# First batch of a fused attention and feed-forward kernel: k and v loaded as two blocks

## The chip, the cores and the metric

One core of a Trainium2 chip runs the whole program. The metric is device time in microseconds (us), a median of several executions. The engines run side by side and wait for each other by semaphores: TensorE (PE in the profile, its weight loads PEld), VectorE (DVE), ScalarE (ACT), GpSimd (POOL) and SyncE (SP). Loads are started by instructions in the queues of SP and ACT and are carried out by 16 DMA engines.

## The reference

For each of 8 batches and 8 heads (576 positions, head size 64, 32 memory slots):

```python
a = exp(phi - max(phi, axis=2));  a = a / (sum(a, axis=2) + 1e-9)
k_m = einsum('bhsm,bhsd->bhmd', a, k)          # 32 x 64 per head
v_m = einsum('bhsm,bhsd->bhmd', a, v)
attn = softmax(q @ k_m.T / sqrt(64))            # 576 x 32 per head
x = (attn @ v_m)  -> rows of 8 * 64 = 512       # 4608 x 512
h = x @ w_in;  g = h * sigmoid(h)               # 4608 x 2048
out = g @ w_out                                 # 4608 x 512
```

## The kernel before, in words

The batches are worked one after the other. For each, the softmax weights of phi are exponentials `e`; matmuls with `e` as weights sum k, v and a column of ones into 32 rows per head (`e_mm`), so that the ones give the sum to divide by. The scores come from q and k's sums, and are turned, exponentiated and normed. v's sums are not multiplied with the scores but with w_in (`p_mm`), and the result is the weight of the first matrix multiplication of the feed-forward part (`ffn1`, line 637). `silu` and `ffn2` (line 676) follow, 16 steps of 128 columns of h for a batch. In steady state TensorE does 12 matmuls of `ffn1` and 12 of `ffn2` for each step, and all that prepares the next batch lies beside them.

The start is written out by hand, from line 768 on, and the change is there. The order of the instructions of TensorE, VectorE, ScalarE and SP is fixed as written (`in_order`). Nothing of the feed-forward part can run before batch 0 has gone through the attention, and the loop for batch 0 also loads and converts the rest of the weights. The weights come as 64-bit words; `w_conv` makes float32 of them in steps that are single letters: "p" and "c" on ScalarE, "s" and "a" on VectorE, for w_out also "h" and "l". `keep_warm` issues matmuls whose result nobody reads.

The steps that the prediction names, in the order of the code:

- `load_phi`, `load_kv`: phi in three pieces; k, v and ones of batch 0 interleaved in one array, 129 columns for each head and position, four loads of 516 KB (128 positions each) and one of 258 KB (the last 64 positions, `kr`), all on ACT's queue.
- `LOADS` (line 43): the loads after these, on SP's queue: i0 and i1 are the first two 128-column blocks of w_in (512 KB each), Q0 and Q1 the halves of q (576 KB each), o0 and o1 blocks of w_out (512 KB each), L the next weights in a list. Each of them waits until the load five places before it has landed (`DEEP`).
- `phi_max` to `phi_exp`: the exponentials of the two head groups p = 0 and p = 1, in this order.
- `e_mm(0)`: for p = 0, then p = 1, 16 matmuls of 129 columns (lines 318 to 323), and 16 for the last 64 positions (line 330); then the sums of the ones, their reciprocals (`rs`), and the scaled k and v (`kvn`).
- `f_tr`, `f_vt`: transposes of k's and v's part of `kvn`, copied by VectorE and ScalarE into `kvT`.
- `f_scores(u)`, `f_copy(u)`, `f_turn(u)` for the two halves u of q: scores (line 480), copies to SBUF (`sT`, `sleft`), transposes back (`firstu`).
- `f_max`, `f_sub`, `f_exp`, `f_sum`, `f_norm`, `f_back`, `f_high`, `f_low`: the softmax and its split into two parts, `aparts`. `f_high(1)` is the last that the first matmuls of `ffn1` wait for.
- `p_mm(0, 0)` needs v's part of `kvT` and the converted i0 and i1.

The lines that set the order around the change:

```python
LOADS = "i0 Q0 Q1 i1 o0 o1 L L L"
...
        e_mm(0)
        w_conv(I0, 0, "pc")
        keep_warm(idle, 3)
        f_tr()
        f_vt()
...
        f_scores(1)
        f_max(0)
        f_copy(1)
        f_sub(0)
        keep_warm(spare, 3)
        f_turn(1)
```

Of the kernel before, what the change touches and what calls it, by code (L numbers as in the profile page):

```python
# [10 lines left out]
F32 = mybir.dt.float32  # L11
# [4 lines left out]
AF = mybir.ActivationFunctionType  # L16
ALU = mybir.AluOpType
AX = mybir.AxisListType

P = 128  # L20
B, S, H, M, D = 8, 576, 8, 32, 64
# [17 lines left out]

PHW = FULLC * HM + P  # L40
KVC = 2 * NR * KVW
RAWB = 3
LOADS = "i0 Q0 Q1 i1 o0 o1 L L L"
HOMES = {("o", 1): 8, ("i", 2): 12}
DEEP = 5

# [2 lines left out]
def attn_ffn_kernel(  # L49
    ctx: ExitStack,  # L50
    tc: tile.TileContext,
    phi: bass.AP,
    kv: bass.AP,
    qT: bass.AP,
    w_in: bass.AP,
# [126 lines left out]
    def load_next(few=False):  # L182
        w = next(to_load, None)
        if w is not None:
            w_load(w, None, few)
# [35 lines left out]
    def load_kv(b):  # L221
        queue = nc.scalar if b == 0 else None
        ts = []
        for c in range(FULLC):
            t = sb.tile([P, 2, NR, KVW], F32, tag="kv", name=f"kv{b}_{c}", bufs=FULLC)
            load(t.rearrange("p g r f -> p (g r f)"), kv[b, :, c * KVC : (c + 1) * KVC], queue=queue)
            ts.append(t)
        t = sb.tile([P, NR, KVW], F32, tag="kr", name=f"kr{b}", bufs=1)
        load(t.rearrange("p r f -> p (r f)"), kv[b, :, FULLC * KVC :], queue=queue)
        at[b]["kv"], at[b]["kr"] = ts, t  # L230

    def load_q(b, hf, few=False):
        t = sb.tile([P, NR, HALF], F32, tag="q", name=f"q{b}_{hf}", bufs=2)
        at[b]["q", hf] = t
        load(t.rearrange("p r s -> p (r s)"), qT[b, hf], few)
# [78 lines left out]
    def e_mm(b):  # L314
# [26 lines left out]
        for p in range(2):  # L341
# [3 lines left out]
            else:  # L345
                nc.vector.tensor_scalar(kvn[:, :, p], src, rs[p], None, op0=ALU.mult)

    def e_tr(b):
        pt = beside_h(P)
        t = sb.tile([P, 2, NR, M], F32, tag="kvT", name=f"kvT{b}", bufs=2)  # L350
        for kind in range(2):
            nc.tensor.transpose(pt[kind], kvn[:, kind].rearrange("p g d -> p (g d)"), ident)  # L352
        nc.vector.tensor_copy(t[:, 0].rearrange("p r m -> p (r m)"), pt[0])
        nc.scalar.copy(t[:, 1].rearrange("p r m -> p (r m)"), pt[1])
        at[b]["kvT"] = t
# [100 lines left out]
    def f_tr():  # L456
        pt = ps.tile([P, 512], F32, tag="acc", name="firstt", bufs=NI)
        t = sb.tile([P, 2, NR, M], F32, tag="kvT", name="kvT0", bufs=2)
        at[0]["kvT"] = t
        for kind in range(2):  # L460
            nc.tensor.transpose(
                pt[:, P * kind : P * (kind + 1)], kvn[:, kind].rearrange("p g d -> p (g d)"), ident
            )
        nc.vector.tensor_copy(t[:, 0].rearrange("p r m -> p (r m)"), pt[:, :P])
        first["vt"] = t, pt

    def f_vt():
        t, pt = first["vt"]
        nc.scalar.copy(t[:, 1].rearrange("p r m -> p (r m)"), pt[:, P : 2 * P])

    def f_scores(u):
        if u == 0:
# [15 lines left out]
    def f_copy(u):  # L488
        if u == 0:
            first["left"] = sb.tile([P, P], F32, tag="mx", name="sleft", bufs=1)  # L490
        t = first["main", u] = sb.tile([P, 2, 2 * P], F32, tag="kv", name=f"sT{u}", bufs=FULLC)
        left = first["left"].rearrange("p (g h f) -> p g h f", g=2, h=2)[:, :, u]
        st = first["st", u]
        if u:
            nc.scalar.copy(t, st[:, :, : 2 * P])
            nc.scalar.copy(left, st[:, :, 2 * P : HALF])
            return
        nc.scalar.copy(t[:, 0], st[0][:, : 2 * P])
        nc.vector.tensor_copy(t[:, 1], st[1][:, : 2 * P])
        for p in range(2):  # L500
            nc.scalar.copy(left[:, p], st[p][:, 2 * P : HALF])
# [43 lines left out]
    def f_exp(u):  # L545
        nc.scalar.activation(f_sc(u), f_sc(u), AF.Exp, scale=SCALE)
# [221 lines left out]
    with in_order(DVE, ACT) as last:  # L768
        load_phi(0)
        nc.scalar.activation(tiny[:, :1], ident[:, :1], AF.Exp)  # L770
        load_kv(0)
        for c in LOADS.split():
            if c[0] == "Q":
                load_q(0, int(c[1]), True)
            elif c[0] == "L":
                load_next(True)
            else:
                w_load((c[0], 0), int(c[1]), True)
        keep_warm(idle, 10)
# [7 lines left out]
        for p in range(2):  # L787
            phi_exp(0, (p,))
        keep_warm(idle, 2)
        e_mm(0)  # L790
        w_conv(I0, 0, "pc")
        keep_warm(idle, 3)
        f_tr()
        f_vt()
        w_conv(I0, 0, "s")
        keep_warm(idle, 2)
        f_scores(0)
# [6 lines left out]
        f_max(0)  # L804
        f_copy(1)
        f_sub(0)
        keep_warm(spare, 3)
        f_turn(1)
        f_exp(0)
        w_conv(I0, 1, "pc")  # L810
        f_max(1)
        f_sub(1)
        f_exp(1)
        nc.scalar.activation(tiny[:, :1], ident[:, :1], AF.Silu)
        keep_warm(spare, 13)
        f_sum(0)
        f_norm(0)
        w_conv(I0, 1, "sa")
# [110 lines left out]
def layout(q, k, v, phi, moe_w_in, moe_w_out):  # L929
# [7 lines left out]
        ],  # L937
        axis=2,
    )
    ph = phi.reshape(B, NR, 2, S, M).transpose(0, 3, 2, 1, 4).reshape(B, S, 2, P)  # L940
    ph = np.concatenate(
        [
# [10 lines left out]
    qT = q[:, :, cols].reshape(B, NR, 2, 2, HALF, D).transpose(0, 3, 2, 5, 1, 4).reshape(B, 2, P, NR * HALF)  # L953
    return {
        "in_phi": np.ascontiguousarray(ph),
        "in_kv": np.ascontiguousarray(kv),
        "in_q": np.ascontiguousarray(qT),
        "in_w_in": np.ascontiguousarray(moe_w_in).view(np.int64),
# [12 lines left out]
```

## Time and profile before

| | us |
|---|---|
| median of 3 runs | 701.22 (701.16 to 701.29) |
| the profiled execution | 702.12 |
| its span, first to last instruction | 700.3 |
| TensorE busy in it | 689.4 |
| VectorE busy | 365.4 |
| ScalarE busy | 259.0 |

Times in the rows below are microseconds from the span's start, unless ns stands beside them. The profiled execution is 0.90 us longer than the median of the runs.

### The profile page before, as it was taken

Reading aid. Unit: us, or ns where it says so; the run is one execution under the profiler, and the core shown is the slowest. Engines: PE = TensorE matmul, PEld = TensorE weight load, DVE = VectorE, ACT = ScalarE, POOL = GpSimd, SP = SyncE. Lnnn points to the kernel's source line nnn. Section 1 sums busy time; section 2 is a strip of 40 time slices with the busy share of each in tenths; the row PEclk is TensorE's granted clock in tenths of the full one; section 3 lists DMA queues with packets and bytes.
Section 4 is the critical chain, followed back from the end, with each engine's and each line's share of the span. In section 5 each row is a group of like instructions: output and inputs, shape, how many; then the busy total and the mean of one; then the engine's idle time right before and its main releaser. Section 6 shows DMA issues by size and latency. Waiting matters only on the chain.

```text
span 700.3 us, 11773 instructions
## 1 busy us (share of the span) xinstructions
PE 689.4 (98%) x4924; PEld 562.4 (80%) x4924; DVE 365.4 (52%) x665; ACT 259.0 (37%) x456; POOL 0.7 (0%) x6
## 2 busy tenths in 40 slices
PE   7999999999999999999999999999999999999997
PEld 3578777888888888888888888888888888888886
DVE  4898797435654256534636346542564525623322
ACT  3879584422424224421423314342241413431211
POOL 0000000000000000000000000000000000000000
PEclk9999999999999999999999999999999999999999
DMA  9995752212201221132110311112121000010002
GB/s 334 317 338 187 254 212 95 78 61 68 92 19 46 92 68 44 52 137 69 35 61 16 137 56 47 61 54 83 68 80 31 1 1 1 1 61 1 1 0 76
DMA packets 25445, 60.15 MB, mean 86 GB/s; under 512 B 2096, under 2 KB 10416, under 8 KB 25392
## 3 DMA queue, kind: packets, MB, share of 16 engines
q1 hardware_dynamic: 24448, 56.63, 22.8%
q10 hardware_dynamic: 944, 2.77, 1.1%
q8 instruction: 39, 0.64, 0.4%
q14 instruction: 14, 0.11, 0.1%
HBM read 49.95 MB, written 9.44 MB: 85 GB/s over the span
## 4 chain that ended last, share of the span: by engine, by line
PE 84%; DVE 2%; issue 0%; ACT 0%; ACTq 0%
PE acc L676 45%; PE h L637 25%; PE accleft L676 6%; PE bg L602 4%; PE h L322 2%; PE bg L367 1%; DVE wo_lo L176 0%; DVE raw L172 0%; PE h L330 0%; PE h L352 0%; DVE aparts L448 0%; DVE aT L442 0%; DVE gparts L654 0%; DVE sc L415 0%; DVE smx L411 0%
## 5 line engine op out<-in xcount | busy, mean ns | idle before, releaser
L676 PE MATMUL acc<-wo_hi,gparts 128*128 128x512 f32 x1024 | 341.8, 395 | 0.1
L676 PEld LDWEIGHTS acc<-wo_hi,gparts 128*128 128x128 f32 x1024 | 192.0, 188 | 52.7 <-issue 6.6
L637 PEld LDWEIGHTS h<-aparts,pparts 128*128 128x128 f32 x1524 | 214.0, 188 | 14.4 <-issue 2.1
L637 PE MATMUL h<-aparts,pparts 128*128 128x288 f32 x1524 | 223.3, 295 | 0.7 <-ACT aparts L581 0.4
L660 ACT ACTIVATE g<-h 128x512 f32<-128x512 f32 x127 | 76.0, 599 | 345.9 <-PE h L637 180.3
L676 PE MATMUL acc<-wo_lo,gparts 128*128 128x512 f32 x512 | 200.8, 392 | 0.7 <-DVE wo_lo L176 0.6
L652 DVE CAST gparts<-g 128x512 fp32r<-128x512 f32 x128 | 54.4, 425 | 260.0 <-ACT g L660 260.0
L676 PEld LDWEIGHTS acc<-wo_lo,gparts 128*128 128x128 f32 x512 | 96.1, 188 | 18.4 <-DVE wo_lo L176 1.9
L654 DVE TENSOR_TENSOR gparts<-g,gparts 128x512 fp32r<-128x512 f32 x128 | 88.2, 689 | 10.3
L618 DVE TENSOR_TENSOR pparts<-bg,pparts 128x1024 fp32r<-128x1024 f32 (+1 forms) x36 | 39.7, 1102 | 5.4 <-ACT pparts L616 5.0
L676 PE MATMUL accleft<-wo_hi,gparts 128*128 128x512 f32 x128 | 40.6, 389 | 0.0
L616 ACT ACTIVATE pparts<-bg 128x1024 fp32r<-128x1024 f32 (+1 forms) x36 | 33.6, 932 | 14.8 <-PE bg L602 14.8
L602 PE MATMUL bg<-win,kvT 64*32 64x512 f32 (+1 forms) x576 | 35.8, 554 | 0.0
L676 PEld LDWEIGHTS accleft<-wo_hi,gparts 128*128 128x128 f32 x128 | 24.0, 188 | 4.9
L662 ACT ACTIVATE gleft<-h 128x64 f32<-128x64 f32 x127 | 27.8, 219 | 0.0
L683 ACT ACTIVATE o<-acc 128x512 f32<-128x512 f32 x32 | 19.2, 600 | 21.8 <-PE acc L676 10.6
L676 PE MATMUL accleft<-wo_lo,gparts 128*128 128x512 f32 x64 | 24.9, 389 | 0.0
L660 ACT ACT_TABLE_LOAD x14 | 18.0, 1283 | 14.2 <-issue 13.6
L652 DVE CAST gparts<-gleft 128x512 fp32r<-128x512 f32 x16 | 6.8, 427 | 20.7 <-PE accleft L676 12.2
L168 ACT ACTIVATE raw<-raw 128x1024 int32<-128x1024 uint32 (+1 forms) x16 | 16.8, 1048 | 0.0
L322 PEld LDWEIGHTS h<-kv,phi 128*32 128x32 f32 x384 | 10.2, 110 | 5.0 <-ACT gleft L662 5.0
L676 PEld LDWEIGHTS accleft<-wo_lo,gparts 128*128 128x128 f32 x64 | 12.0, 188 | 2.4
(139 smaller groups left out, 365.0 us busy)
## 6 DMA issues: line engine op xcount, KB each, us to landing
kv<-in_kv SPq DMA_DIRECT2D x28, 516.0 KB, 5.9
q<-in_q SPq DMA_DIRECT2D x16, 576.0 KB, 5.7
out<-o SPq DMA_DIRECT2D x32, 256.0 KB, 2.1
raw<-in_w_in SPq DMA_DIRECT2D x14, 512.0 KB, 6.6
raw<-in_w_out SPq DMA_DIRECT2D x6, 1024.0 KB, 5.5
phi<-in_phi SPq DMA_DIRECT2D x7, 576.0 KB, 3.8
kv<-in_kv ACTq DMA_DIRECT2D x4, 516.0 KB, 6.8
kr<-in_kv SPq DMA_DIRECT2D x7, 258.0 KB, 6.4
```

What stands on the lines that cost most here:

```text
L168: nc.scalar.activation(r, low, AF.Copy, scale=2.0**-29)
L322: nc.tensor.matmul(pt[p][M * r : M * (r + 1), :KVW], e[:, p, c, M * r : M * (r + 1)], kvt[c][:, p, r], start=c == 0, stop=False, skip_grou ...
L602: nc.tensor.matmul(bg[M * r : M * (r + 1), p, :w].rearrange("p (k f) -> p k f", f=P), kvT[D * p : D * (p + 1), 1, r], win[D * p : D * (p + ...
L616: nc.scalar.activation(hi[:, :, c], bg[:, :, :w], AF.Copy)
L618: nc.vector.tensor_tensor(lo[:, :, c], bg[:, :, :w], hi[:, :, c], op=ALU.subtract)
L637: nc.tensor.matmul(h[:, hf, :HALF], wt[:, p, fs], a[:, p, hf * HALF : (hf + 1) * HALF], start=n[hf] == 0, stop=n[hf] == 5, skip_group_chec ...
L652: nc.vector.tensor_copy(ghi, g32)
L654: last_split.append(nc.vector.tensor_tensor(glo, g32, ghi, op=ALU.subtract))
L660: nc.scalar.activation(g32.rearrange("p (h f) -> p h f", h=2), h[:, :, :w], AF.Silu)
L662: i = nc.scalar.activation(gleft[:, fc, o : o + LEFT].rearrange("p (h f) -> p h f", h=2), h[:, :, w:HALF], AF.Silu)
L676: nc.tensor.matmul(acc[key], gt[:, cs], wt[:, fc], start=fc == 0 and n == 0, stop=fc == NFC - 1 and n == 2)
L683: nc.scalar.activation(o, a, AF.Copy)
```

## The change

For batch 0 alone, the host lays out a second array of k and v, `kv0`: all of k with its column of ones first (four blocks of 128 positions, then the last 64), then all of v. The loads write into the same tiles as before, k's part ahead of v's part in each. k's five loads (four of 260 KB, one of 130 KB) take the place of the five on ACT's queue. v's five (four of 256 KB, one of 128 KB) go on SP's queue at the place V of `LOADS`, and wait like the others there for the load five places before. The order on SP becomes Q0, i0, Q1, v, i1 and on.

`e_mm(0)` becomes `e_first(0)`, which sums k and the ones (65 columns), and two calls of `e_first(1)`, which sum v (64 columns): p = 0 between `f_scores(1)` and `f_turn(1)` where three `keep_warm` matmuls were, p = 1 behind `f_turn(1)`. Each is 16 matmuls and 4 for the last positions. `k_first` makes `rs` and k's `kvn`, for p = 0 on VectorE and for p = 1 on ScalarE; `v_first` scales v on ScalarE for both p, behind `w_conv(I0, 1, "pc")`. `f_tr` has one transpose. `f_vt` has v's, on TensorE behind three `keep_warm` matmuls after `f_exp(1)`, and its copy on ScalarE ahead of the tiny Silu activation. The 13 `keep_warm` matmuls there become 6. The copies `sT` get other buffers, those that the conversion of w_out uses later.

```diff
--- before.py
+++ after.py
@@ -39,8 +39,11 @@
 
 PHW = FULLC * HM + P
 KVC = 2 * NR * KVW
+KW = D + 1
+KC = 2 * NR * KW
+K0 = FULLC * KC + NR * KW
 RAWB = 3
-LOADS = "i0 Q0 Q1 i1 o0 o1 L L L"
+LOADS = "Q0 i0 Q1 V i1 o0 o1 L L L"
 HOMES = {("o", 1): 8, ("i", 2): 12}
 DEEP = 5
 
...
@@ -228,6 +232,24 @@
         t = sb.tile([P, NR, KVW], F32, tag="kr", name=f"kr{b}", bufs=1)
         load(t.rearrange("p r f -> p (r f)"), kv[b, :, FULLC * KVC :], queue=queue)
         at[b]["kv"], at[b]["kr"] = ts, t
+
+    def kv0_parts(t, n):
+
+        f = t.rearrange("p g r f -> p (g r f)") if n == 2 * NR else t.rearrange("p r f -> p (r f)")
+        k, v = f[:, : n * KW], f[:, n * KW :]
+        return (k, v), (k.rearrange("p (n f) -> p n f", f=KW), v.rearrange("p (n f) -> p n f", f=D))
+
+    def load_kv0(part):
+        if not part:
+            ts = [sb.tile([P, 2, NR, KVW], F32, tag="kv", name=f"kv0_{c}", bufs=FULLC) for c in range(FULLC)]
+            t = sb.tile([P, NR, KVW], F32, tag="kr", name="kr0", bufs=1)
+            at[0]["kv"], at[0]["kr"] = ts, t
+        at_ = part * K0
+        for t, n in [(t, 2 * NR) for t in at[0]["kv"]] + [(at[0]["kr"], NR)]:
+            x = kv0_parts(t, n)[0][part]
+            w = x.shape[-1]
+            load(x, kv0[:, at_ : at_ + w], part == 1, queue=None if part else nc.scalar)
+            at_ += w
 
     def load_q(b, hf, few=False):
         t = sb.tile([P, NR, HALF], F32, tag="q", name=f"q{b}_{hf}", bufs=2)
@@ -345,6 +367,45 @@
             else:
                 nc.vector.tensor_scalar(kvn[:, :, p], src, rs[p], None, op0=ALU.mult)
 
+    def e_first(part, pt, ps_):
+
+        e, er, kvt, kr = (at[0][k] for k in ("e", "er", "kv", "kr"))
+        w = (KW, D)[part]
+        at[0]["ep", part] = pt
+        for p in ps_:
+            for c in range(FULLC):
+                x = kv0_parts(kvt[c], 2 * NR)[1][part]
+                for r in range(NR):
+                    nc.tensor.matmul(
+                        pt[p][M * r : M * (r + 1), :w],
+                        e[:, p, c, M * r : M * (r + 1)],
+                        x[:, p * NR + r],
+                        start=c == 0, stop=False, skip_group_check=True,
+                    )
+            x = kv0_parts(kr, NR)[1][part]
+            for r in range(NR):
+                nc.tensor.matmul(
+                    pt[p][M * r : M * (r + 1), :w],
+                    er[rows(p), M * r : M * (r + 1)],
+                    x[rows(p), r],
+                    start=False, stop=True, skip_group_check=True,
+                )
+
+    def k_first():
+        pt = at[0]["ep", 0]
+        rs = at[0]["rs"] = [sb.tile([P, 1], F32, tag="rs", name="rs", bufs=2) for p in range(2)]
+        for p in range(2):
+            nc.vector.tensor_scalar(rs[p], pt[p][:, D:KW], EPS, None, op0=ALU.add)
+            nc.vector.reciprocal(rs[p], rs[p])
+            if p:
+                nc.scalar.activation(kvn[:, 0, p], pt[p][:, :D], AF.Copy, scale=rs[p])
+            else:
+                nc.vector.tensor_scalar(kvn[:, 0, p], pt[p][:, :D], rs[p], None, op0=ALU.mult)
+
+    def v_first():
+        for p in range(2):
+            nc.scalar.activation(kvn[:, 1, p], at[0]["ep", 1][p][:, :D], AF.Copy, scale=at[0]["rs"][p])
+
     def e_tr(b):
         pt = beside_h(P)
         t = sb.tile([P, 2, NR, M], F32, tag="kvT", name=f"kvT{b}", bufs=2)
@@ -457,16 +518,13 @@
         pt = ps.tile([P, 512], F32, tag="acc", name="firstt", bufs=NI)
         t = sb.tile([P, 2, NR, M], F32, tag="kvT", name="kvT0", bufs=2)
         at[0]["kvT"] = t
-        for kind in range(2):
-            nc.tensor.transpose(
-                pt[:, P * kind : P * (kind + 1)], kvn[:, kind].rearrange("p g d -> p (g d)"), ident
-            )
+        nc.tensor.transpose(pt[:, :P], kvn[:, 0].rearrange("p g d -> p (g d)"), ident)
         nc.vector.tensor_copy(t[:, 0].rearrange("p r m -> p (r m)"), pt[:, :P])
-        first["vt"] = t, pt
-
-    def f_vt():
-        t, pt = first["vt"]
-        nc.scalar.copy(t[:, 1].rearrange("p r m -> p (r m)"), pt[:, P : 2 * P])
+
+    def f_vt(bg):
+        pt, t = bg[:, 0, P : 2 * P], at[0]["kvT"]
+        nc.tensor.transpose(pt, kvn[:, 1].rearrange("p g d -> p (g d)"), ident)
+        nc.scalar.copy(t[:, 1].rearrange("p r m -> p (r m)"), pt)
 
     def f_scores(u):
         if u == 0:
@@ -488,7 +546,8 @@
     def f_copy(u):
         if u == 0:
             first["left"] = sb.tile([P, P], F32, tag="mx", name="sleft", bufs=1)
-        t = first["main", u] = sb.tile([P, 2, 2 * P], F32, tag="kv", name=f"sT{u}", bufs=FULLC)
+        t = sb.tile([P, 2 + 2 * u, 2 * P], F32, tag=("cva1", "cva")[u], name=f"sT{u}", bufs=1)
+        t = first["main", u] = t[:, :2]
         left = first["left"].rearrange("p (g h f) -> p g h f", g=2, h=2)[:, :, u]
         st = first["st", u]
         if u:
@@ -768,12 +827,14 @@
     with in_order(DVE, ACT) as last:
         load_phi(0)
         nc.scalar.activation(tiny[:, :1], ident[:, :1], AF.Exp)
-        load_kv(0)
+        load_kv0(0)
         for c in LOADS.split():
             if c[0] == "Q":
                 load_q(0, int(c[1]), True)
             elif c[0] == "L":
                 load_next(True)
+            elif c[0] == "V":
+                load_kv0(1)
             else:
                 w_load((c[0], 0), int(c[1]), True)
         keep_warm(idle, 10)
@@ -787,11 +848,11 @@
         for p in range(2):
             phi_exp(0, (p,))
         keep_warm(idle, 2)
-        e_mm(0)
+        e_first(0, banks(0), (0, 1))
+        k_first()
         w_conv(I0, 0, "pc")
         keep_warm(idle, 3)
         f_tr()
-        f_vt()
         w_conv(I0, 0, "s")
         keep_warm(idle, 2)
         f_scores(0)
@@ -804,15 +865,20 @@
         f_max(0)
         f_copy(1)
         f_sub(0)
-        keep_warm(spare, 3)
+        bg = bgtile()
+        e_first(1, [bg[:, p] for p in range(2)], (0,))
         f_turn(1)
+        e_first(1, [bg[:, p] for p in range(2)], (1,))
         f_exp(0)
         w_conv(I0, 1, "pc")
+        v_first()
         f_max(1)
         f_sub(1)
         f_exp(1)
+        keep_warm(spare, 3)
+        f_vt(bg)
         nc.scalar.activation(tiny[:, :1], ident[:, :1], AF.Silu)
-        keep_warm(spare, 13)
+        keep_warm(spare, 6)
         f_sum(0)
         f_norm(0)
         w_conv(I0, 1, "sa")
@@ -937,6 +1003,12 @@
         ],
         axis=2,
     )
+    kv0 = []
+    for x in (np.concatenate([k[0], np.ones((H, S, 1), k.dtype)], axis=2), v[0]):
+        w = x.shape[-1]
+        x = x.reshape(NR, 2, S, w).transpose(2, 1, 0, 3)
+        kv0.append(x[:n].reshape(P, FULLC * 2 * NR * w))
+        kv0.append(x[n:].transpose(1, 0, 2, 3).reshape(P, NR * w))
     ph = phi.reshape(B, NR, 2, S, M).transpose(0, 3, 2, 1, 4).reshape(B, S, 2, P)
     ph = np.concatenate(
         [
...
```

## Rows read from the trace of the kernel before

**Rows 1.** The page, part 4: shares of the chain that ended last, by engine.
```profile
PE 84%; DVE 2%; issue 0%; ACT 0%; ACTq 0%
```
**Rows 2.** Chain of waits, 12 to 110 us, then whole: start, us, what.
```profile
107.56 1.37 DVE aparts L448
...
108.97 1.60 PE h L637 x10
```
**Rows 3.** Timeline of PE: start, us, engine, line, out<-in, count, [idle before <-releaser].
```profile
42.56 0.50 PE L676 MATMUL acc<-wo_lo,gparts 128*128 128x512 f32 x1 [0.38 <-DVE wo_lo L176]
```
**Rows 4.** Timeline of all engines, 10 to 15 us.
```profile
10.21 0.31 ACT L312 ACTIVATE phi<-phi 64x128 f32<-64x128 f32 x1
...
11.03 1.04 PEld L322 LDWEIGHTS first<-kv,phi 128*32 128x32 f32 x40 [1.28 <-DMA kv<-in_kv]
...
12.26 0.18 PEld L330 LDWEIGHTS first<-kr,phi 64*32 64x32 f32 x16 [0.20 <-DMA kr<-in_kv]
12.27 0.45 PE L330 MATMUL first<-kr,phi 64*32 64x129 f32 x16
...
13.38 0.37 ACT L344 ACTIVATE kvn<-first,rs 128x128 f32<-128x128 f32 x1 [2.87 <-DVE rs L340]
...
13.65 0.65 ACT L166 ACTIVATE win<-raw 128x512 f32<-128x512 f32 x1
...
13.80 0.44 PE L461 MATMUL firstt<-ident,kvn 128*128 128x128 f32 x2 [0.33 <-ACT kvn L344]
...
14.63 0.72 PE L480 MATMUL firsts<-q,kvT 64*32 64x288 f32 x16
14.75 0.27 ACT L469 COPY kvT<-firstt 128x128 f32<-128x128 f32 x1
```
**Rows 5.** DMA issues one at a time: phi, i0, Q0, Q1, i1; KB, us to landing.
```profile
phi<-in_phi SPq DMA_DIRECT2D x1, 64.0 KB, 3.5
...
raw<-in_w_in SPq DMA_DIRECT2D x1, 512.0 KB, 7.0
...
q<-in_q SPq DMA_DIRECT2D x1, 576.0 KB, 6.1
...
q<-in_q SPq DMA_DIRECT2D x1, 576.0 KB, 6.3
...
raw<-in_w_in SPq DMA_DIRECT2D x1, 512.0 KB, 6.2
```
**Rows 6.** Timeline of SP's queue: issue of i0, of Q0 and Q1, of i1.
```profile
5.89 0.39 SPq L87 DMA_DIRECT2D raw<-in_w_in  x1
8.23 1.60 SPq L87 DMA_DIRECT2D q<-in_q  x2
11.00 0.38 SPq L87 DMA_DIRECT2D raw<-in_w_in  x1
```
**Rows 7.** Stretches: length, busy of each engine, granted clock, DMA share, GB/s.
```profile
6.00:9.00 3.00, 2.00 (x10) 1.06 (x10) 2.32 (x8) 0.83 (x2) 0.00 (x0) 1.00 0.98 364
...
17.00:19.00 2.00, 1.89 (x18) 1.00 (x11) 1.11 (x3) 1.70 (x4) 0.00 (x0) 1.00 1.03 396
19.00:21.00 2.00, 2.00 (x12) 0.88 (x10) 1.97 (x3) 1.21 (x3) 0.00 (x0) 1.00 1.08 348
```
**Rows 8.** Timeline of all engines, 17 to 27 us.
```profile
17.75 0.22 ACT L496 COPY sleft<-firsts 128x64 f32<-128x64 f32 x1
...
18.02 0.42 PEld L512 LDWEIGHTS firstu<-ident,sT 128*128 128x128 f32 x4 [0.60 <-ACT sleft L496]
...
18.54 0.65 ACT L166 ACTIVATE win<-raw 128x512 f32<-128x512 f32 x1
...
20.54 0.74 ACT L546 ACTIVATE fsc<-fsc 128x640 f32<-128x640 f32 x1 [0.79 <-DVE fsc L540]
...
23.39 0.81 DVE L550 TENSOR_REDUCE fsm<-fsc 128x20 f32<-128x640 f32 x1
...
26.50 0.28 ACT L581 ACTIVATE aparts<-firstar 128x128 fp32r<-128x128 f32 x1 [0.43 <-PE firstar L571]
```

More of the change, by code (lines that the diff above doesn't have):

```diff
@@ L52, in attn_ffn_kernel @@
     phi: bass.AP,
+    kv0: bass.AP,
     kv: bass.AP,
@@ L955, in layout @@
         "in_phi": np.ascontiguousarray(ph),
+        "in_kv0": np.ascontiguousarray(np.concatenate(kv0, axis=1)),
         "in_kv": np.ascontiguousarray(kv),
```

## The prediction

> **What bounds the kernel now.** I read the chain of waits first. TensorE holds 84% of it [rows 1], so later batches can't hide a late start: whatever batch 0 loses or saves is carried to the end. The chain taken for the first 110 us ends in VectorE's split of batch 1's attention, and from 108.97 us on there is only TensorE [rows 2]. Next I read TensorE's own timeline between 34 and 109 us: its matmuls stand end to end, with a few stalls such as 0.38 us for VectorE's `wo_lo` [rows 3]. So the time is decided by when the feed-forward part of batch 0 starts, and a microsecond saved ahead of it is saved at the end, as long as VectorE, ScalarE and the weights come earlier too.
>
> Then the timeline of the first 30 us, with the question which wait ends last. The exponentials of p = 1 are ready at 10.21 + 0.31 = 10.52, but the sums stand until k and v come: 1.28 us of weight loading idle ends at 11.03 with a landing, and the last block, `kr`, lets the last 16 matmuls start at 12.26 [rows 4]. The sums end at 12.72. So between 10.5 and 12.3 us the stream of loads is the bound. From there it is a chain of small steps: `kvn` to 13.75, transposes, the copy of k's part, and the scores at 14.63 [rows 4]. Q0 lands at 8.23 + 6.1 = 14.3 [rows 5, 6], only 0.3 us before the scores want it. Earlier sums alone would run into q; hence the order of the loads counts as much as the split.
>
> **The change, part by part.**
>
> *k's loads.* Up to `kr`, phi (576 KB) and k with v (2322 KB) are moved, 2898 KB. Afterwards phi and k's sums need 576 + 4 x 260 + 130 = 1746 KB, 1152 KB less. That is 1.18 MB, at the 364 GB/s of the stretch that carries k and v [rows 7] 3.2 us; `kr` landed at 12.1, so k's last piece lands at about 8.9. The bound on the good side is about 8.0, since part of i0 moved in those 12.1 us too. On the bad side, if Q0, now released by the first landing, takes half of the engines while k ends, 576 KB come ahead: 10.5. Even that is no later than the exponentials of p = 1 at 10.52, so they become the bound.
>
> *k's sums.* For p = 1, 20 matmuls remain behind 10.52. Before, 40 weight loads took 1.04 us [rows 4], 26 ns each. The trace has no 65-column matmul: below is half of it, 13 ns, above the same 26 ns, as the weight loads are as many. I take 26: 20 x 0.026 = 0.52, plus 0.27 for the last one's length (the 16 of `kr`: 0.45 less 16 x 0.011 of loading), so the end is near 11.35 instead of 12.72: 1.37 us earlier. p = 0 is done before and its `rs` and `kvn` lie beside p = 1's matmuls. At 13 ns it would be 11.1.
>
> *From the sums to the scores.* This took 14.63 - 12.72 = 1.91 us. One sum and one reciprocal remain behind p = 1 instead of two each, `kvn` on ScalarE has 64 columns instead of 128 (between 0.22 for a 64-column copy [rows 8] and 0.37 [rows 4]; I take 0.27, near the 128-column copy), and one transpose is left of two (0.44 [rows 4]). Together some 0.3 us, 0.1 to 0.4. TensorE's three `keep_warm` matmuls end with `kvn`, so they hide. Scores at 14.63 - 1.37 - 0.3 = about 12.95.
>
> *q and w_in.* Q0 stands behind 1746 KB and its own 576: 2322 KB, less than what stood ahead of the old landing of i0 at 5.89 + 7.0 = 12.9 (3410 KB). At 364 to 396 GB/s the 1088 KB between are 2.8 to 3.1 us: about 10. i0 follows with 512 KB at about 11.4, when ScalarE wants it at 12.0; before, it landed at 12.9 for a use behind 13.75. Q1 lands near 12.9; its scores stand behind those of Q0. So each has a microsecond or so.
>
> *v's loads and sums.* Through v, 4562 KB are moved, exactly what before was moved through Q1, which lands near 9.5 + 6.3 = 15.8 [rows 5, 6]. So v's last piece lands near 15.8; from 15.4 to 16.3 if the last 1152 KB run at 396 or 348 GB/s [rows 7]. The p = 0 sums of v stand in TensorE's queue ahead of `f_turn(1)`, which started at 18.02 behind ScalarE's `sleft` [rows 8]. Shifted by 1.65, it wants to start at 16.35. The p = 0 matmuls of the last block take 0.1 us behind the landing. So this new wait ends with 0.4 us to spare; if v comes at 16.3, it costs some 0.1. What waits behind it is all of the second half of the scores: `f_max(1)` and VectorE's whole row of steps.
>
> *ScalarE.* i1 stands behind the same bytes as before and lands at 11.0 + 6.2 = 17.2 [rows 5, 6]. Its conversion began at 18.54 [rows 8], and shifted at 16.9: 0.3 us of waiting. Behind it come the two new scalings of v, some 0.25 each (0.22 to 0.37 as above), in the 0.79 us that ScalarE idled before `f_exp(1)` [rows 8]. 0.3 + 0.5 = 0.8 just fills it. v's copy, 0.27 [rows 4], moves from 14.75 to behind `f_exp(1)`, where ScalarE runs without idle time until the 0.43 us ahead of 26.50 [rows 8]; those take it. VectorE wants the result of `f_exp(1)` (20.54 + 0.74 = 21.28) only at 23.39 [rows 8], a cover of 2.1 us. If i1 lands 0.5 us later still, half of that shows up at `f_high(1)`; on the other side, nothing is gained.
>
> *The fillers, and SP's five additional issues.* TensorE's fillers are fewer by seven and don't stand on the path. The granted clock reads 1.00 in each stretch [rows 7], the 2.4 GHz level, and v's 40 matmuls fill part of the room. Five issues of about 0.4 us each on SP lie between landings.
>
> *Sum.* -1.37 - 0.3 = -1.67 at the scores; +0.1 for v and ScalarE's additions: -1.6 (bounds: -1.1 to -2.0) at the first `ffn1`. In the profiled execution's own time 702.12 - 1.6 = 700.5; the median of the runs lies 0.90 lower, so 701.22 - 1.6 = 699.6.
>
> **A rule against it.** Rows of k and v, 4128 bytes for a partition, came at 364 GB/s, and the stretch from 17 to 19 us, mostly o0's rows of 4096 bytes, at 396 [rows 7]. The Trainium skill ("DMA: Bandwidth & Descriptors", section "How a descriptor splits into AXI transactions") says that a piece which doesn't start on a multiple of 256 bytes fetches from the multiple below, so that the bytes before it are moved for nothing. The trace agrees in direction. By that rule, as an estimate, rows cut into 2080 and 2048 bytes pay the 112 or so lost bytes twice, 2.7% of 2322 KB more or 0.17 us, and v lands near 16.0; the sum would stay.
>
> **The rivals.**
>
> *v or i1 comes later, and half the gain is spent.* For it: v's blocks are half as large, each issued only when the load five before has landed, and even 64 KB took 3.5 us from issue to landing at the start [rows 5]. Five of 256 KB in 3.5 us are 375 GB/s, hardly what the engines can do. Against it: larger loads stand in the line with them. At 0.8 us late (16.6 for v's end) `f_turn(1)` starts 0.35 later and ScalarE loses 0.5: a gain of 0.9, 700.3.
>
> *The gain is lost in the loop for batch 0.* VectorE stalls TensorE at some steps [rows 3], and if it or the weights don't move along, the stalls grow by what came earlier. Against it: the stalls are few and short. The gain falls to 0.2: 701.0.
>
> *The place of the old wait is taken by v on TensorE: slower.* The order of TensorE is fixed, so `f_turn(1)` and all behind it wait for v's last block. Each microsecond that it lands behind 16.25 goes to the end, and from 17.9 on the kernel is slower than before. If the throttle costs each of the five blocks 0.6 us, v ends at 18.8: 0.9 slower, and with i1 pushed behind by the same bubbles 1.5 slower, 702.7. Against it: 3 us of lost transfer are three times what any stretch of the trace shows.
>
> *The split does nothing,* because k's sums wait for all of the tile that v is loaded into. They would then start at 15.8 and end at 16.2, 3.5 later than before, 704.7. Against it: i0's conversion started at 13.65 [rows 4], long before i1, the other half of the same tile, landed at 17.2 [rows 5, 6].
>
> **How the numbers follow.** Forecast 55%, v or i1 late 17%, lost in the loop 11%, v as the new wait 13%, the split without effect 4%. A difference of 0.2% is 1.4 us, about what a measurement can tell. Of the forecast's 55, 40 lie above a gain of 1.4, and 2 of the second case: faster 42%. Slower by over 1.4 are the last case and 7 of the 13, and 1 of the loop's: 12%. The rest, 46%, is within. The range reaches from a gain of 2.4, a little past the bounds of the sum, to 0.6 slower: 698.8 to 701.8, leaving out the last two cases for the most part.
>
> **What would show it.** The last of k's sums should end near 11.35 without a wait for k's loads, the scores start near 12.95, v's last load land near 15.8, `f_turn(1)` start near 16.4 behind ScalarE and not behind v's landing, and `f_high(2)`, the step at 26.50 [rows 8], come 1.6 earlier. Wrong would be a long wait of v's matmuls for a landing, or a `f_high(2)` that is early while the steady state, from 108.97 on before, is not.

## The result, and the profile after

The kernel after takes 703.39 us (median of 8 runs, 702.32 to 704.08), the kernel before in the same comparison 701.44 (8 runs, 701.16 to 701.73). The ratio on record, which isn't that of the two medians, is 1.0024, 95% interval 1.0015 to 1.0033: 0.24% slower, where a gain of 1.6 us was forecast. Of the runs below, one execution each of e9, e10 and the kernel before took 1372 to 3853 us; the ratios leave them out, and as e10's is its profiled one, nothing is read from that trace. The profiled execution is 703.40 with a span of 701.6; before it was 702.12 and 700.3.

The chain of waits is still TensorE's, at 82% where [rows 1] has 84%:

```profile
PE 82%; DVE 3%; issue 1%; ACT 1%; DMA 0%; ACTq 0%
```

The timeline of the kernel after (start, length, engine, line, operation, and in brackets the idle time before with what ended it) tells the whole case, from the first sums to the steady state:

```profile
11.01 0.32 PE L387 MATMUL first<-kr,phi 64*32 64x65 f32 x8
...
12.93 0.72 PE L538 MATMUL firsts<-q,kvT 64*32 64x288 f32 x16
...
16.43 0.32 PE L379 MATMUL bg<-kv,phi 128*32 128x64 f32 x8 [0.61 <-DMA kv<-in_kv]
...
17.12 0.32 PE L379 MATMUL bg<-kv,phi 128*32 128x64 f32 x8 [0.36 <-DMA kv<-in_kv]
17.49 0.15 PEld L387 LDWEIGHTS bg<-kr,phi 64*32 64x32 f32 x8 [0.22 <-DMA kr<-in_kv]
...
17.73 0.42 PEld L571 LDWEIGHTS firstu<-ident,sT 128*128 128x128 f32 x4
...
19.42 0.67 ACT L170 ACTIVATE win<-raw 128x512 f32<-128x512 f32 x1 [2.49 <-DMA raw<-in_w_in]
...
25.86 0.27 PE L630 MATMUL firstar<-ident,fsc 128*128 128x128 f32 x1
...
26.57 1.12 ACT L170 ACTIVATE win<-raw 128x1024 f32<-128x1024 f32 x1 [1.14 <-DMA raw<-in_w_in]
27.60 0.27 ACT L640 ACTIVATE aparts<-firstar 128x128 fp32r<-128x128 f32 x1
...
27.92 2.21 PE L696 MATMUL h<-aparts,pparts 128*128 128x288 f32 x12 [1.78 <-ACT aparts L640]
...
110.09 1.60 PE L696 MATMUL h<-aparts,pparts 128*128 128x288 f32 x10 [0.27 <-DVE aparts L509]
```

k's sums end at 11.33 and the scores start at 12.93, 1.70 us ahead of [rows 4]. Then v's sums wait three times for a landing, the last until 17.49, and `f_turn(1)` starts at 17.73 where [rows 8] has 18.02: of 1.70 us 0.29 are left. ScalarE waits 2.49 us for i1, whose conversion starts 0.88 later than before. The last piece, `firstar`, is ready at 26.13, but ScalarE has to convert I1 (the next two 128-column blocks of w_in, the first L of `LOADS`) before `f_high(2)`, in its fixed order, and I1 lands at 26.57: `f_high(2)` stands at 27.60 (before 26.50). TensorE takes that over as 1.09 us at the first `ffn1`, and 1.12 at the step that was at 108.97 [rows 2]; the span is 1.3 longer. In the kernel before, I1's conversion waited for nothing (its second half was issued at 15.80, took 7.5 us and so had landed at 23.3):

```profile
24.93 1.14 ACT L166 ACTIVATE win<-raw 128x1024 f32<-128x1024 f32 x1
...
26.83 2.21 PE L637 MATMUL h<-aparts,pparts 128*128 128x288 f32 x12 [0.37 <-ACT aparts L581]
```

Why the loads are late is read from two more views: SP's queue (start of the issue, how long SP held it, what is loaded, how many) and then the stretches (length, busy time of PE, PEld, DVE, ACT, POOL, granted clock, DMA share, GB/s).

```profile
5.28 0.33 SPq L91 DMA_DIRECT2D q<-in_q  x1
6.58 0.39 SPq L91 DMA_DIRECT2D raw<-in_w_in  x1
7.31 0.34 SPq L91 DMA_DIRECT2D q<-in_q  x1
7.93 4.69 SPq L91 DMA_DIRECT2D kv<-in_kv  x4
13.75 0.33 SPq L91 DMA_DIRECT2D kr<-in_kv  x1
14.40 0.77 SPq L91 DMA_DIRECT2D raw<-in_w_in  x1
...
17.09 1.04 SPq L91 DMA_DIRECT2D raw<-in_w_in  x2
```

```profile
6.00:10.00 4.00, 2.84 (x47) 1.69 (x50) 3.24 (x9) 1.10 (x3) 0.00 (x0) 1.00 0.97 318
10.00:14.00 4.00, 3.69 (x72) 1.50 (x72) 1.89 (x9) 2.52 (x6) 0.00 (x0) 1.00 1.04 384
14.00:18.00 4.00, 2.97 (x63) 1.61 (x63) 2.18 (x4) 1.71 (x6) 0.00 (x0) 1.00 0.79 256
18.00:22.00 4.00, 2.98 (x53) 1.66 (x52) 3.33 (x7) 2.56 (x7) 0.00 (x0) 1.00 0.98 302
```

The kernel before moved 368 and 398 GB/s in the first two, and in the others:

```profile
14.00:18.00 4.00, 3.91 (x45) 1.27 (x44) 3.03 (x6) 2.37 (x8) 0.00 (x0) 1.00 1.04 389
18.00:22.00 4.00, 3.57 (x18) 1.77 (x18) 3.04 (x6) 3.19 (x5) 0.00 (x0) 1.00 1.06 360
```

The five-deep wait counts loads, not bytes. Each landing of a k block, of Q0 or of i0 lets only 256 KB of v in, and v's last 128 KB wait for Q1: issued at 7.31, 6.4 us to its landing, so 13.75. By then only blocks of 256 and 128 KB are under way, and i1 and o0 wait for v's first two. The DMA share falls to 0.79 (before 1.04), and the loads behind are issued late. 14 to 22 us move 0.76 MB less than before, (389 - 256 + 360 - 302) GB/s x 4 us, which is 2 us of a full stream; the 50 GB/s missing from 6 to 10 us are another 0.2 MB.

### The profile page after: what moved, and what is told of

It reads as the page before. It is cut to its first block, busy times and chain, and to the rows that moved or that the text cites. A ratio compares the mean times of both kernels' runs of the same rounds, so it can differ in the third digit from the quotient of the medians.

```text
span 701.6 us, 11918 instructions
## 1 busy us (share of the span) xinstructions
PE 689.5 (98%) x4997; PEld 562.7 (80%) x4997; DVE 365.9 (52%) x665; ACT 259.4 (37%) x458; POOL 0.7 (0%) x6
## 4 chain that ended last, share of the span: by engine, by line
PE 82%; DVE 3%; issue 1%; ACT 1%; DMA 0%; ACTq 0%
PE acc L735 44%; PE h L696 25%; PE accleft L735 6%; PE bg L661 4%; PE h L344 2%; PE bg L428 1%; DMA out<-o 0%; DVE gparts L713 0%; DVE wo_lo L180 0%; DVE raw L176 0%; PE h L352 0%; PE h L413 0%; DVE gparts L711 0%; DVE pparts L677 0%; DVE aparts L509 0%
## 5 line engine op out<-in xcount | busy, mean ns | idle before, releaser
L696 PEld LDWEIGHTS h<-aparts,pparts 128*128 128x128 f32 x1524 | 214.0, 188 | 15.8 <-issue 2.9
L742 ACT ACTIVATE o<-acc 128x512 f32<-128x512 f32 x32 | 19.1, 598 | 19.8 <-PE acc L735 10.6
```

Of the source, the lines that this page charges most:

```text
L696: nc.tensor.matmul(h[:, hf, :HALF], wt[:, p, fs], a[:, p, hf * HALF : (hf + 1) * HALF], start=n[hf] == 0, stop=n[hf] == 5, skip_group_chec ...
L742: nc.scalar.activation(o, a, AF.Copy)
```

## The experiments

The theories, with the letters that the expectations use. A: too few bytes are in flight behind v's small blocks. B: the short rows of k's and v's blocks are slow in themselves, however many are in flight. C: the late landings belong to the one execution that was profiled. D: what turns the late loads into a loss is ScalarE's order, I1's conversion ahead of `f_high`. E, against D: v's landing alone decides, and I1's lies beside it. F: the longer wait of TensorE costs granted clock afterwards. G: v's own small blocks, one after the other on SP's queue, keep v late. Each group of runs below shared its runs of the kernel before; runs of different groups are compared through the ratio to it.

**e0: the kernel after, unchanged.**

> The changed kernel once more, to see how much of its profile is chance. Theory A (five loads in flight are too few bytes once v comes in blocks of 256 KB, so the DMA engines run dry and v and all weights behind it land late): again 703.4 (702.3 to 704.1), and again stretches far below 364 GB/s between 14 and 22 us, v's last landing after 17 us, I1's after 26. Theory B (the stream is slower throughout because rows of 2080 and 2048 bytes take longer for each byte): 703.4 as well, but with an even loss. Theory C (a disturbed execution was profiled): the low stretches are gone or lie elsewhere.

703.25 us, ratio 1.0017 [1.0009, 1.0026]. 14 to 18 us moved 271 GB/s and 18 to 22 us 265: the holes are the kernel's, and C falls. TensorE was hardly busy from 26 to 28 us, and then the granted clock fell, as the stretches of e0 show (the last three columns are clock, DMA share and GB/s):

```profile
26.00:28.00 2.00, 0.37 (x3) 0.19 (x2) 0.89 (x2) 1.53 (x3) 0.00 (x0) 1.00 1.03 378
...
29.00:30.00 1.00, 1.00 (x6) 0.91 (x5) 1.00 (x3) 0.00 (x0) 0.00 (x0) 0.56 1.11 351
30.00:31.00 1.00, 1.00 (x6) 1.00 (x5) 0.38 (x1) 0.41 (x1) 0.00 (x0) 0.50 1.10 349
31.00:32.00 1.00, 1.00 (x6) 1.00 (x5) 0.78 (x2) 1.00 (x3) 0.00 (x0) 0.50 1.09 349
```

0.50 is the 1.2 GHz level. In the profile of the kernel after, TensorE was busy for 0.22 us of the same two, and the clock stayed at 1.00 from 28 to 32 us; so the wait alone doesn't decide it. `ffn1` started at 27.82, 0.10 before that of the profile above, and the step of 110.09 came at 110.70, 0.61 after it.

**e1: eight deep from v's first load on.**

```diff
-                loads[-DEEP].ins.name,
+                loads[-(8 if len(loads) > 10 else DEEP)].ins.name,
```

> The changed kernel, but v's five loads and all behind them wait for the load eight places before instead of five; order, sizes and rows are unchanged. Theory A: v lands near 15.8, the second turn starts near 16.4, I1 no longer holds ScalarE, 699.6 to 700.4. Theory B: no change, 703.4.

701.49 us, 0.9994 [0.9986, 1.0003], 1.76 less than e0. Stretches and then timeline of e1:

```profile
14.00:18.00 4.00, 3.19 (x65) 1.88 (x65) 2.09 (x4) 1.66 (x6) 0.00 (x0) 1.00 1.06 385
18.00:22.00 4.00, 3.46 (x55) 1.80 (x54) 3.70 (x7) 3.42 (x7) 0.00 (x0) 1.00 1.07 375
```

```profile
17.11 0.15 PEld L387 LDWEIGHTS bg<-kr,phi 64*32 64x32 f32 x8 [0.23 <-DMA kr<-in_kv]
...
18.57 0.67 ACT L170 ACTIVATE win<-raw 128x512 f32<-128x512 f32 x1 [1.58 <-DMA raw<-in_w_in]
...
24.90 1.16 ACT L170 ACTIVATE win<-raw 128x1024 f32<-128x1024 f32 x1 [0.31 <-DMA raw<-in_w_in]
25.96 0.26 ACT L640 ACTIVATE aparts<-firstar 128x128 fp32r<-128x128 f32 x1
```

The same rows now come at 385 GB/s, so B isn't the main cause of the hole at 14 to 22 us, and A is. v's last block still comes at 17.11 and not at 15.8, and the time misses A's 699.6 to 700.4: the repair brings the kernel back to before, not to the forecast. From 4 to 14 us 0.4 MB less are moved than in the kernel before (327, 313 and 361 GB/s from 4, 6 and 10 us on, against 349, 368 and 398), which is 1.1 us at 385 GB/s. The depth doesn't repair that part.

**e2: v as one load of 1024 KB and one of 128** (into the not yet used `win[:, 4:8]`).

```diff
+        if part:
+            w = FULLC * 2 * NR * D
+            at[0]["v"] = win[:, 4:8].rearrange("p k r f -> p (k r f)")
+            load(at[0]["v"], kv0[:, K0 : K0 + w], True)
+            load(kv0_parts(at[0]["kr"], NR)[0][1], kv0[:, K0 + w :], True)
+            return
...
```

> The changed kernel, but v comes in two loads, 1024 KB and 128 KB, into a stretch of w_in's buffer that is free then; each load still waits for the one five places before. Theory A: with the bytes in flight restored 699.6 to 700.6. Theory B: rows of 8192 bytes repair v's part of the loss and not k's, so about half of the loss is left, 701.5 to 702.5.

702.58 us, 1.0007 [0.9998, 1.0016]. 14 to 18 us are whole again at 389 GB/s, but v's sums now wait for the whole megabyte, until 17.26, the next stretch moves 332, and the granted clock reads 0.61 in it. The time misses A's 699.6 to 700.6 and lies just above B's 701.5 to 702.5; by itself e2 doesn't tell the two apart.

**e3: the kernel before, three deep.**

```diff
-DEEP = 5
+DEEP = 3
```

> The kernel before, but each load of the list waits for the load three places before instead of five; k and v together as before. Theory A: three loads of 512 to 576 KB are about the bytes of five with 256 KB blocks among them, so low stretches appear and it loses 0.7 to 2.5 us: 702.1 to 704. Theory B: unchanged, 701.4.

706.51 us, 1.0062 [1.0049, 1.0075], 4.4 us slower, more than any theory had. 10 to 14 us move 272 GB/s, and the scores wait for q:

```profile
16.39 1.22 PE L480 MATMUL firsts<-q,kvT 64*32 64x288 f32 x16 [2.21 <-DMA q<-in_q]
```

Fewer bytes in flight make the loads of the kernel before late too, without v's split and short rows. The 4.4 us aren't late loads alone: with TensorE busy for 1.79 of the 4 us from 14 to 18, the granted clock reads 0.77 there and 0.80 from 18 to 22 us.

**e4 and e7: eight deep for all loads,** after and before (`DEEP = 8`).

> The changed kernel with all loads of the list eight deep, Q0, i0 and Q1 too. With eight deep from v on, the stretch from 14 to 22 us was mended (375 to 385 GB/s), while 6 to 10 us stayed at 313 GB/s against 368 before, and v's last block landed at 17.1. Theory A (too few bytes in flight): that stretch mends as well, v lands near 16.2, 1.2 to 1.8 below the kernel before of the same call. Theory B (short rows of k take longer): 6 to 10 us stays near 315 GB/s and the time stays 0.6 below. If Q0 takes half the engines from k, k's sums wait for k beyond 10.5 us and it is not better than 0.3 below.

> The kernel before with the list eight deep. Theory A: its loads of 512 KB and more keep the engines busy at five already (360 to 400 GB/s in each stretch), so within 0.3 of the kernel before. If a deeper list were worth something by itself, apart from the change, it would be 0.5 to 1 below.

705.45 us, 1.0046 [1.0034, 1.0059], and 708.98, 1.0096 [1.0080, 1.0111]: both much slower, both for a reason that no theory had named. In e4's timeline, then in e7's:

```profile
9.14 0.34 ACTq L91 DMA_DIRECT2D kr<-in_kv  x1
9.52 0.63 ACT L333 ACTIVATE phi<-phi 128x512 f32<-128x512 f32 x1 [6.84 <-DMA kv<-in_kv]
...
14.55 0.44 PE L387 MATMUL first<-kr,phi 64*32 64x65 f32 x8 [2.32 <-DMA kr<-in_kv]
```

```profile
13.77 0.33 ACTq L87 DMA_DIRECT2D kr<-in_kv  x1
14.21 0.63 ACT L311 ACTIVATE phi<-phi 128x512 f32<-128x512 f32 x1 [11.53 <-DMA q<-in_q]
...
18.69 0.46 PE L330 MATMUL first<-kr,phi 64*32 64x129 f32 x16 [0.48 <-DMA kr<-in_kv]
```

The last load on ACT's own queue is issued only after the landing of a load on SP's queue, and ScalarE's exponentials stand behind it. In the traces of all these programs the issues of loads and stores name eight completion semaphores in turn, 16 or 17 issues each. In both runs this `kr` takes the one that Q0 had taken at 4.11 (e4) and 4.73 (e7), and it is issued when Q0 has landed, 5.0 and 9.0 us later (the bracket of e4 names another load). So in these programs eight in flight is a limit whatever `DEEP` says, and an issue waits for whoever had its semaphore before. The granted clock fell in both as well, to 0.51 (e4) and 0.54 (e7) from 14 to 18 us. e4 says nothing on A.

**e5 and e15: I1's conversion behind `f_high(1)`,** in the kernel after and, as a control, in the kernel before.

```diff
-        w_conv(I1, None, "p")
         f_norm(1)
...
         f_high(1)
+        w_conv(I1, None, "p")
```

> The changed kernel, five deep, with ScalarE's first step of I1's conversion (1.12 us, which waited for I1's landing) moved behind f_high(1). Theory D (two waits: v's landing on TensorE takes 1.4 of the 1.7 gained, and I1's landing, in ScalarE's order ahead of f_high, makes it slower than before): the first feed-forward matmuls come 0.8 to 1.3 earlier, 0.5 to 1.2 below the changed kernel, 702.1 to 702.8 where that is 703.25. Rival E (v's wait alone decides, I1's lies beside it): no change, or up to 0.5 slower since I1 is needed soon after.

> The kernel before with I1's first step moved behind f_high(1), as a control. Theory D (the move helped the changed kernel by 1.7 because I1 landed late there): here I1 lands in time, no gain beyond 0.3, or up to 0.5 slower. If the move is worth 0.8 or more here as well, it says nothing on the late landing.

e5: 701.58 us, 0.9991 [0.9983, 1.0000]; e15: 701.89, 0.9997 [0.9988, 1.0006]. Timeline of e5:

```profile
18.56 0.15 PEld L387 LDWEIGHTS bg<-kr,phi 64*32 64x32 f32 x8 [0.32 <-DMA kr<-in_kv]
...
27.23 0.28 ACT L640 ACTIVATE aparts<-firstar 128x128 fp32r<-128x128 f32 x1 [1.12 <-PE firstar L630]
...
28.14 1.16 ACT L170 ACTIVATE win<-raw 128x1024 f32<-128x1024 f32 x1
```

The loads came even later in this execution (v at 18.56), but `f_high(2)` waits for TensorE now and no longer for I1. The first `ffn1` stood at 27.56, 0.36 earlier than in the kernel after, the steady state at 109.19, 0.90 earlier; the ratio falls by 0.26 percentage points against e0's, 1.8 us, more than the 0.5 to 1.2 expected. D holds, and E falls. The move gives the kernel before nothing measurable, where I1 was converted at 24.93; so what it takes away is a loss that the change had made.

**e6: v's loads right behind k's on ACT's queue,** without the wait.

```diff
-LOADS = "Q0 i0 Q1 V i1 o0 o1 L L L"
+LOADS = "Q0 i0 Q1 i1 o0 o1 L L L"
...
-            load(x, kv0[:, at_ : at_ + w], part == 1, queue=None if part else nc.scalar)
+            load(x, kv0[:, at_ : at_ + w], queue=nc.scalar)
...
+        load_kv0(1)
```

> The changed kernel with v's five loads right behind k's on ACT's queue, without the wait for earlier landings; then Q0, i0, Q1 and the rest, five deep. v's sums stay where they are. Theory A with fixed order: v has landed by 13 and never waits, k's sums still end near 11.4, but Q0 lands near 13.2 and i0 near 14.5, for which ScalarE waits ahead of the scores' copies: gain 0 to 0.4 against the kernel before. If v's place in TensorE's order and not its landing were the fault, it would stay 1 above.

705.90 us, 1.0049 [1.0036, 1.0062]: a miss. The first stretch of e6 shows the short rows at full speed, the second what it cost:

```profile
6.00:10.00 4.00, 2.93 (x50) 1.72 (x50) 3.21 (x9) 1.20 (x3) 0.00 (x0) 1.00 1.03 374
18.00:22.00 4.00, 4.00 (x64) 2.42 (x63) 1.43 (x3) 2.11 (x5) 0.00 (x0) 0.50 1.05 393
```

374 GB/s, where the kernel before moved 368, speaks against B once more. But Q0 is issued at 9.64, i0's conversion waits until 16.00, and from 18 to 22 us TensorE runs at the 1.2 GHz level.

**e8, e9, e10: deeper earlier, and the move.** e8 waits six deep for Q0, i0 and Q1 and eight behind; e9 is e1 with e5's move, e10 is e8 with it.

```diff
-                loads[-DEEP].ins.name,
+                loads[-(8 if len(loads) > 10 else 6)].ins.name,
```

> The changed kernel with Q0, i0 and Q1 six deep and v and all behind it eight deep; here k's last load on ACT's queue waits only for a piece of phi, as in the changed kernel. (All eight deep was slow for another reason: k's last load had to wait for loads of the list, with ScalarE's exponentials queued behind it.) Theory A (too few bytes in flight): the stretch from 6 to 10 us, 313 GB/s with five deep there, rises above 340, v lands by 16.6, 0.9 to 1.6 below the kernel before. Theory B (short rows of k): as with five and eight, 0.6 below.

> The changed kernel with v and all behind it eight deep, and I1's first step moved behind f_high(1). Apart they were 1.8 and 1.7 below the changed kernel. If both repair the consequence of the same late loads, together they are 2.0 to 2.9 below it, 1.0 to 1.6 below the kernel before, and the bound is then v's landing at about 17; if I1's landing was all that counted, not better than either alone, 0.6 below.

> Both depths, six and eight, and I1's step moved: the version that the runs point to. Theory A: v near 16.5 and neither wait left, 1.2 to 1.8 below the kernel before, the gain that was forecast. If k is held up by Q0 or the loads stay late, no better than 1.0 below.

702.78 us, 1.0011 [1.0002, 1.0019]; 701.24, 0.9993 [0.9984, 1.0002]; 702.02, 1.0001 [0.9992, 1.0010]. None has the gain that A expected. e9 fits the other case named for it, not better than either repair alone, and e10 too, no better than 1.0 below. e8 moves 354 GB/s from 6 to 10 us, but e0 and e9, five deep there, move 353 and 349; so it isn't shown that the sixth load lifts it. SP holds v's first load until 10.42, v ends at 16.88 and I1 lands at 25.03. In that execution (701.84) the first `ffn1` is at 26.39, 0.44 earlier than before; why e8's median lies higher its trace doesn't show. e9 is the fastest median of the study and yet no better than before beyond the interval; e1's and e5's repairs don't add up, since with I1 early there is little left to move (in e1 `f_high(2)` starts 0.22 us after `firstar` is ready).

**e11: 13 fillers instead of 5 ahead of `f_back(1)`,** against F.

```diff
-        keep_warm(spare, 5)
+        keep_warm(spare, 13)
```

> The changed kernel, five deep, with 13 fillers instead of 5 ahead of the second group of transposes, where TensorE stood idle from 26 to 28 us and a profile showed a granted clock of 0.50 from 29 to 33 us afterwards. Theory F (the waits also cost clock in some executions, about 1.5 us in those): all executions at a mean clock of 0.998 or more, none above 703.6, median 0.3 to 0.6 below the changed kernel's, 702.6 to 703.0 where that is 703.25. Rival: the clock has no part in it, and the spread stays from 702 to 704.8.

704.66 us, 1.0034 [1.0024, 1.0044]. The fillers got into the path, as the timeline of e11 shows:

```profile
24.61 2.98 PE L83 MATMUL spare<-ident 128*128 128x512 bf16 x13
...
27.43 0.60 PE L622 MATMUL firsta<-ident,fsc 128*128 128x128 f32 x4
```

The transposes stood at 25.43 without them. The mean clocks of its executions read 0.997 to 1.000, e0's 0.996 to 1.000, and the ratio is above e0's 1.0017: the expectation is missed, and the run says nothing on how much the clock costs.

**e12, e13, e14: larger loads.** e12 loads k as one block of 1040 KB (into `win[:, 3:8]`) and the last 130 KB; e13 also v as one of 1024 KB (into `gleft`) and the last 128; e14 is e13 with the move.

```diff
+        if not part:
+            w = FULLC * KC
+            at[0]["k"] = win[:, 3:8].rearrange("p k r f -> p (k r f)")[:, :w]
+            load(at[0]["k"], kv0[:, :w], queue=nc.scalar)
...
+        at[0]["v"] = gleft.rearrange("p k f -> p (k f)")
+        load(at[0]["v"], kv0[:, K0 : K0 + w], True)
...
```

> The changed kernel, five deep, with k's four loads of 260 KB made one of 1040 KB into a stretch of w_in's buffer that is free then; v's five loads as in the change. The list then stands two blocks of v further ahead in bytes, k's rows are 8320 bytes. Theory A (bytes in flight): early stretches at 340 GB/s or more, v's last block by 16.5, 0.6 to 1.4 below the kernel before. Rival G (v's own small blocks, one after the other on SP's queue, keep it late): v at 17 or later, within 0.5 of the kernel before or slower.

> The changed kernel, five deep, with k as one load of 1040 KB and v as one of 1024 KB, each with its small last block. Theory A: 1.0 to 1.7 below the kernel before, v's sums at 16.2 or earlier. Rival G would be mended by this too; what speaks against both is v's sums still waiting until 17, and a time within 0.5 of the kernel before: then it is the total bytes ahead of v that land later than forecast, whatever the size of the loads.

> As with k and v as one load each, with I1's first step moved behind f_high(1). Theory A and D: 1.2 to 1.8 below the kernel before, 0 to 0.5 below the same without the move, since I1 lands nearly in time.

702.89 us, 1.0014 [1.0005, 1.0024]; 701.79, 1.0002 [0.9991, 1.0013]; 701.73, 1.0000 [0.9989, 1.0011]: all three times miss the gain of 0.6 us and more that A had expected. With k alone in one block the hole at 14 to 18 us stays (267 GB/s), as A has it, since v's blocks are still small. But more was moved before (390 GB/s from 4 to 6 us), v's sums never wait for v, the last of them standing at 16.14, and G falls. I1 is late all the same, and holds `f_high(2)` until 26.31 where `firstar` is ready at 24.92, which is D with v in time:

```profile
25.30 1.12 ACT L170 ACTIVATE win<-raw 128x1024 f32<-128x1024 f32 x1 [1.07 <-DMA raw<-in_w_in]
```

With both in one block the hole is gone (382), and the profiled execution of e13, 700.21 us with a span of 698.4, shows what the split does when the loads come:

```profile
16.03 0.15 PEld L399 LDWEIGHTS bg<-kr,phi 64*32 64x32 f32 x8 [0.43 <-DMA kr<-in_kv]
...
17.49 0.67 ACT L170 ACTIVATE win<-raw 128x512 f32<-128x512 f32 x1 [0.86 <-DMA raw<-in_w_in]
...
23.39 1.17 ACT L170 ACTIVATE win<-raw 128x1024 f32<-128x1024 f32 x1
...
25.03 2.22 PE L708 MATMUL h<-aparts,pparts 128*128 128x288 f32 x12 [0.37 <-ACT aparts L652]
...
107.16 1.60 PE L708 MATMUL h<-aparts,pparts 128*128 128x288 f32 x10 [0.27 <-DVE aparts L521]
```

The first `ffn1` is 1.80 us earlier than before and the steady state 1.81: the forecast's gain, in one execution. e14's profiled one, 700.49, is like it, with the first `ffn1` at 25.20. But the twelve of e13 lie between 700.21 and 704.93, and the medians of both gain nothing.

## Why the prediction was wrong

**The step that failed** is "v's last piece lands near 15.8; from 15.4 to 16.3 if the last 1152 KB run at 396 or 348 GB/s". It took the place of v in the list for its time, on the ground that the same bytes stand ahead. The bytes were right; the rates were those of a list of 512 KB loads. The loads ahead of v were late already: Q0 landed at 10.6, i0 at 12.3 and Q1 at 13.7, where about 10, 11.4 and 12.9 were forecast. v's last block landed near 17.45 (issued 13.75, 3.7 us), at 256 GB/s in the last stretch. The same step carries i1 (17.2 forecast from [rows 5, 6], 19.4 measured) and, not written down at all, I1, which the kernel before converted at 24.93 and this one at 26.57. The prediction had seen the cause, "Five of 256 KB in 3.5 us are 375 GB/s", but with a time from issue to landing that belonged to a 64 KB load; v's own four took 6.1 us, and five of 256 KB in 6.1 us are 215 GB/s, a sixth under what was measured. e1 repairs the 14 to 22 us and 1.8 us of time by the depth alone; that is the cause shown for the hole and the loss. e2, e3 and e13 agree: larger loads close the hole, a shallower list opens one in the kernel before. For the 0.8 us that Q1 was late no run shows the cause.

The rule of the Trainium skill weighed in the prediction ("DMA: Bandwidth & Descriptors", section "How a descriptor splits into AXI transactions": a piece that doesn't start on a multiple of 256 bytes also fetches the bytes below it) gave an estimate of 0.17 us for the cut rows. v was 1.65 us late; e1's rows are the same ones, so what they cost is within the 1.3 us that e1 leaves, and no run tested them alone.

**The second step that failed** is the cover on ScalarE. The text counted i1 and `f_exp(1)`, "0.3 + 0.5 = 0.8 just fills it", and took `f_high(2)` to follow. It left out that I1's conversion stands ahead of `f_high(2)` in the same order. I1 had landed 1.6 us ahead of its conversion in the kernel before, just the gain that was forecast, so any lateness would show. That is what turned a gain of 0.29 at `f_turn(1)` into a loss of 1.10 at `f_high(2)`, as e5 with its control e15 shows.

**What was right.** k's sums (11.35 forecast, 11.33 measured), scores (12.95, 12.93), q in time, the parts of a tile independent of each other, and the carrying of a difference at the first `ffn1` to the end (1.09, 1.12, span 1.3). That k's sums came so close is partly luck. The trace has two records for each of these matmuls (40 for the 20 of p = 1, and the 16 of `kr` in the kernel before are 8 matmuls), so "20 x 0.026" priced half of them; against that a record took 16 ns (0.50 us for 32) and not 26, and the matmuls began at 10.42, while the last exponentials still ran (to 10.70, and not to 10.52). The sum for a list that comes in time held in the profiled execution of e13 (-1.80 at the first `ffn1` for -1.6), but in no median. Of the rivals it was "the place of the old wait is taken by v on TensorE", with its i1 "pushed behind by the same bubbles", 702.7, and given 13%. It had the mechanism, but priced the bubbles as unlikely, "three times what any stretch of the trace shows": a trace of a list of large loads can't show what small ones do. Its place of the loss was off: v alone only spent the gain, I1 made the loss.

**What stays open.** Why no median reaches the gain that single executions of e13 and e14 show, with v and I1 in time. Executions of the changed kernels scatter more: the kernel before 0.6 us in the result's 8 runs and 0.8 to 2.8 in the 15 to 35 of each group, after 1.8, e0 2.8, e13 4.7. The early loads scatter too, with the same loads up to Q1: from 6 to 10 us 304 to 353 GB/s in seven profiles (the kernel after, e0, e1, e2, e5, e9, e11), where the kernel before and e15 move 368 and 373. That the one makes the other isn't shown. In e0 the three with a mean clock of 0.997 or less are the three longest, 704.03 to 704.82, but in the eight runs of the result one with a mean clock of 1.000 took 703.85; so the clock is a part of it at most. Why 4 to 6 us move 288 to 355 GB/s with k in 260 KB blocks (the same seven) and 390 to 410 with k in one (e12 to e14) isn't settled between the length of the rows and the bytes in flight. In e5 and e9 the loop of batch 0 from the first `ffn1` to the steady state takes 81.6 us instead of 82.1, in e14 and e15, which have the same move, not; why stays open.

## What to carry to other kernels

A throttle that counts loads is tuned for their size: when a load is cut in two, either raise the count with it or count bytes, and price the new landing from the bytes that the list lets into flight, not from those ahead. Where an engine's order is fixed, follow every load that is consumed ahead of the critical step, also those far behind the change. A gain ahead of a chain is worth what the latest of its other inputs leaves.

## What the runs showed of the hardware

- With v in loads of 256 and 128 KB, five deep moved 256 to 274 GB/s at 14 to 18 us (the kernel after, e0, e5, e11, e12), eight deep 381 and 385 (e9, e1), and one load of 1024 KB for v, five deep, 375 to 389 (e2, e13, e14). e8, eight deep with v's first load issued only at 10.42, moved 316.
- An issue on ACT's queue was held until the landing of a load on SP's that had the same completion semaphore (at 9.14 and 13.77 in e4 and e7), and all of ScalarE's work behind it with it.
- After TensorE had been busy for 0.37 of 2 us, its granted clock went from 1.00 to 0.50 at 29 us for about 3 us (e0), while another execution of the same kernel, busy for 0.22 of the same 2 us, read 1.00 (the kernel after).
